# Moving transposes from TensorE to a DMA queue in a fused attention and expert kernel

**Chip, cores, metric.** One core of a Trainium2 chip. The time is device microseconds (us) of the core, the median of several executions. Engines are named as in the profile: PE (TensorE), PEld (its weight loads), DVE (VectorE), ACT (ScalarE), POOL (GpSimd), SP (SyncE, which here only issues DMAs). The profile gives the time of every DMA queue as a share of the same 16 DMA engines of the core.

## The reference

Pooled attention, then a routing by domain to eight experts. The result of the attention is the input of the experts.

```python
q_pool = q.reshape(B, H, S // 2, 2, D).mean(axis=3)        # B = H = 8, S = 1152, D = 64
scores = scale * np.matmul(q_pool, k.transpose(0, 1, 3, 2))
attn = softmax(scores)                                     # (cut: max, exp, sum)
x = np.matmul(attn, v).transpose(0, 2, 1, 3).reshape(4608, 512)
for e in range(8):
    mask = domain_id == e                                  # w1[e]: 512 x 1024, w2[e]: 1024 x 512
    out[mask] = np.maximum(x[mask] @ w1[e], 0.0) @ w2[e]
```

## The kernel before

Attention works on 32 pairs of heads. A pair is 12 steps; a step is one score block on PE (128 x 864) and its exponential on ACT. Keys and queries lie with tokens on partitions when they are loaded, and the kernel's score matmuls read them turned, so PE transposes them into PSUM and DVE copies them out:

```python
def turn_k(p):                       # eight key blocks; turn_q(p) does the ninth and six query blocks
    mt = tpsum.tile([P, 1024], F16, name="tp")
    for c in range(8):
        nc.tensor.transpose(mt[:, c * P : (c + 1) * P], in_=kp[:, c, :, :]..., identity=ident16[:, :])
    nc.vector.tensor_copy(kq[p][:, 0 : 8 * P], mt[:, :])
```

The main loop, one turn per step `t` (cut):

```python
p, s_ = divmod(t, SPP)                              # pair, step in the pair
if s_ == 0: load_q(p + 2)                           # SP's queue, 590 KB
if s_ in (2, 6): (load_k if s_ == 2 else load_v)(p + 3)   # GpSimd's software queue, cast to 16 bits
score(t); expo(t)
...                                                 # values of earlier steps, stores of x to DRAM
if s_ == 3: turn_k(p + 1)
if s_ == 7: turn_q(p + 1)
...                                                 # fills: expert tiles of 128 tokens where PE has room
if s_ == 8: prep_q(p + 2)                           # DVE: sum of the query pairs
if s_ == 11: prep_k(p + 2)                          # DVE: reorder
if t in WANT: want_weights(WANT.index(t))           # four experts' weights, 2.1 MB each
```

Rows of x go to DRAM, are gathered by expert (GpSimd), transposed by PE, and multiplied. There are 40 such tiles; 6 are done inside attention, 34 in a tail after it, in runs of up to five tiles of one expert (a run of the tail is tiles that use the same weights, one after the other). In the tail, short runs (up to 512 columns) share one PSUM tile between two row blocks:

```python
if m > 512:       hp_ = hps.tile([P, 1024], FP32, name="hp")       # hps: two buffers
elif f % 2 == 0:  hb_ = hps.tile([P, 1024], FP32, name="hp"); hp_ = hb_[:, 0:512]
else:             hp_ = hb_[:, 512:1024]
```

The softmax here doesn't subtract the row's maximum and nothing guards it: scores larger than these inputs give would overflow.

## Time and profile before

| | before |
|---|---|
| time, median of 4 (range) | 475.20 us (473.92 to 476.79) |
| attention ends (last exponential) | 319.5 us |
| last matmul of the tail | 466.3 us |
| tiles inside attention / in the tail | 6 / 34 |

The prediction below shows the busy shares, the slices and the waits.

### The profile page before, as it was taken

The page shows a single profiled execution, that of the slowest core. Times are in us where ns is not written, and L with a number is a line of the kernel's source. Part 1 is how long each engine was busy: PE and PEld are TensorE (multiplying, and loading weights), DVE is VectorE, ACT ScalarE, POOL GpSimd, SP SyncE. Part 2 cuts the span into 40 slices and gives each one's busy share as a digit, 9 for nine tenths or more (in the row PEclk, how much of TensorE's full clock was granted, in tenths as well). Part 3 has the DMA queues.
Part 4 walks back from the last instruction along what each step waited for, and adds up shares of the span by engine and source line. Part 5 has one row for each costly group of instructions (what it writes and reads, how often), then busy time and mean ns, then how long its engine had stood idle before and what let it go on. Part 6 is the DMA issues. An engine that isn't in the chain of part 4 may idle for free.

```text
span 473.8 us, 13280 instructions
## 1 busy us (share of the span) xinstructions
PE 443.1 (94%) x5683; PEld 313.9 (66%) x5683; DVE 227.8 (48%) x572; ACT 348.0 (73%) x459; POOL 161.4 (34%) x271
## 2 busy tenths in 40 slices
PE   7999999999999999999999999996888879999993
PEld 4777777877877877777787787773444445555551
DVE  4488778876454554554455454433222223232230
ACT  3999999999999999999999999991222223223220
POOL 4311231222611304564512432003336675533313
PEclk9999999999999999999999999998999999999998
DMA  9995699999999788599978666003219999912203
GB/s 204 219 245 90 129 240 221 183 260 189 167 244 227 121 201 185 100 200 276 244 124 207 138 120 150 1 25 96 80 58 169 217 222 222 232 58 84 81 16 109
DMA packets 48904, 75.23 MB, mean 159 GB/s; under 512 B 5567, under 2 KB 35008, under 8 KB 48834
## 3 DMA queue, kind: packets, MB, share of 16 engines
q0 software_dynamic: 35056, 50.05, 55.2%
q1 hardware_dynamic: 13186, 23.83, 18.6%
q8 instruction: 46, 0.75, 0.7%
q10 hardware_dynamic: 592, 0.39, 0.3%
q14 instruction: 24, 0.20, 0.1%
HBM read 95.46 MB, written 15.21 MB: 234 GB/s over the span
## 4 chain that ended last, share of the span: by engine, by line
ACT 52%; PE 26%; issue 11%; POOL 6%; DMA 3%; DVE 1%; POOLq 1%; ACTq 0%
ACT e L599 49%; PE s L587 8%; PE hp L1010 5%; PE op L1031 4%; PE acc L610 4%; POOL out_dram L504 4%; DMA w2h<-in_moe_w_dram 3%; ACT hT L1015 2%; PE m L763 1%; POOL xs L648 1%; PE m L776 1%; PE tp L550 1%; PE xp L985 1%; PE tp L564 0%; PE acc L161 0%
## 5 line engine op out<-in xcount | busy, mean ns | idle before, releaser
L599 ACT ACTIVATE e<-s 128x864 f16<-128x864 f32 x384 | 305.8, 893 | 4.7 <-PE s L587 3.9
L587 PE MATMUL s<-qz,kq 128*128 128x432 f16 (+2 forms) x1152 | 202.9, 284 | 5.6 <-ACT e L599 3.7
L610 PEld LDWEIGHTS <-e 128*128 128x128 f16 x2880 | 120.6, 97 | 24.7 <-DVE xb L624 7.8
L610 PE MATMUL acc<-v,e 128*128 128x65 f16 x2880 | 134.2, 193 | 0.3 <-ACT e L599 0.3
L587 PEld LDWEIGHTS <-kq 128*128 128x128 f16 x1152 | 97.9, 97 | 30.6 <-issue 10.2
L504 POOL DMA_INDIRECT out_dram<-osb,gid x40 | 40.2, 1004 | 102.9 <-ACT osb L1037 46.4
L648 POOL DMA_INDIRECT xs<-x_tok,grow x40 | 42.1, 1053 | 73.3 <-DVE xs L92 48.7
L1010 PE MATMUL hp<-xt,w1h 128*128 128x128 f16 (+3 forms) x384 | 57.7, 303 | 8.9 <-ACT hT L1015 8.9
L112 POOL DMA_DIRECT2D vs<-in_v_dram x32 | 23.9, 745 | 116.3 <-DVE v L529 57.1
L1031 PE MATMUL op<-w2h,hT 128*128 128x512 f16 x272 | 63.4, 379 | 0.0
L1010 PEld LDWEIGHTS <-w1h 128*128 128x128 f16 x416 | 35.9, 98 | 41.2 <-issue 17.5
L1015 ACT ACTIVATE hT<-hp 128x384 f16<-128x384 f32 (+2 forms) x36 | 20.7, 574 | 49.5 <-PE hp L1010 49.4
L1017 DVE TENSOR_SCALAR hT<-hp 128x384 f16<-128x384 f32 (+2 forms) x36 | 23.8, 661 | 65.1 <-PE hp L1010 63.6
L571 DVE COPY qz<-tp 64x576 f16<-64x576 f16 x62 | 28.2, 455 | 55.1 <-PE tp L564 51.1
L1037 ACT COPY osb<-op 128x512 f32<-128x512 f32 x21 | 12.3, 586 | 55.7 <-PE op L1031 50.0
L1031 PEld LDWEIGHTS <-hT 128*128 128x128 f16 x272 | 25.4, 98 | 25.2
L623 DVE RECIPROCAL rr<-acc 128x10 f32<-128x10 f32 x32 | 7.1, 221 | 48.1 <-PE acc L610 48.0
L520 DVE TENSOR_TENSOR qp<-q 96x768 f16<-96x768 f32 x31 | 29.3, 946 | 0.0
L624 DVE TENSOR_TENSOR xb<-acc,rr 128x640 f16<-128x640 f32 x32 | 26.4, 824 | 1.1
L1039 DVE COPY osb<-op 128x512 f32<-128x512 f32 x13 | 9.0, 692 | 35.5 <-PE op L1031 26.7
L121 POOL DMA_DIRECT2D k<-in_k_dram x31 | 23.3, 752 | 6.6 <-DVE q L92 3.6
L554 DVE COPY kq<-tp 128x1024 f16<-128x1024 f16 x31 | 21.2, 684 | 2.8 <-PE tp L550 2.7
(134 smaller groups left out, 323.2 us busy)
## 6 DMA issues: line engine op xcount, KB each, us to landing
q<-in_q_dram SPq DMA_DIRECT2D x30, 576.0 KB
vs<-in_v_dram POOLq DMA_DIRECT2D x32, 288.0 KB
k<-in_k_dram POOLq DMA_DIRECT2D x31, 288.0 KB
w1h<-in_moe_w_dram POOLq DMA_DIRECT2D x16, 512.0 KB
w2h<-in_moe_w_dram POOLq DMA_DIRECT2D x16, 512.0 KB
x_tok<-xb SPq DMA_DIRECT2D x23, 96.0 KB
x_tok<-xb SPq DMA_DIRECT2D x22, 64.0 KB
q<-in_q_dram SPq DMA_DIRECT2D x4, 288.0 KB
```

What stands on the lines that cost most here:

```text
L112: nc.gpsimd.dma_start(vs[:, :, :, :], v[b, h : h + 2].rearrange("h (p c) d -> p h c d", p=P))
L504: ins = nc.gpsimd.indirect_dma_start(out=dst[:, :], out_offset=bass.IndirectOffsetOnAxis(ap=ap, axis=0), in_=src, in_offset=None, **kw,)
L520: nc.vector.tensor_tensor(out=qp[:, :, :, :].rearrange("p j h d -> p h j d"), in0=q2[:, :, :, 0:D], in1=q2[:, :, :, D : 2 * D], op=ALU.add,)
L571: nc.vector.tensor_copy(qz[p % 2][r][lo : lo + 64, :], mt[lo : lo + 64, P : P + Sp])
L587: nc.tensor.matmul(s[:, r, o : o + n], lhsT=kq[p][:, c * P : (c + 1) * P], rhs=qz[p % 2][r][:, q0 : q0 + n], start=True, stop=True,)
L599: nc.scalar.activation(e_[:, :, o : o + W], st.pop(t)[:, :, 0:W], AF.Exp, bias=0.0, scale=0.0625)
L610: nc.tensor.matmul(acc[p][:, h, i * (D + 1) : (i + 1) * (D + 1)], lhsT=e_[:, h, o + QO[i] : o + QO[i] + P], rhs=v16[p % NV][:, c, h, 0 : D ...
L624: nc.vector.tensor_tensor(out=xb[b][:, :, 2 * hp * D : 2 * (hp + 1) * D].rearrange("p i (h d) -> p h i d", h=2), in0=a[:, :, :, 0:D], in1= ...
L648: nc.gpsimd.indirect_dma_start(out=dst, out_offset=None, in_=x_dram[0 : 1 + nb * Sp, :], in_offset=bass.IndirectOffsetOnAxis(ap=ap, axis=0),)
L1010: nc.tensor.matmul(hp_[:, lo : lo + n], lhsT=w1h[:, cc, f * P : (f + 1) * P], rhs=xt[:, cc, lo : lo + n], start=cc == 0, stop=cc == ND - 1,)
L1015: nc.scalar.activation(hT[:, f, 0:m], hp_[:, 0:m], AF.Relu)
L1031: nc.tensor.matmul(op_[:, :], lhsT=hT[:, f, i * P : (i + 1) * P], rhs=w2h[:, f, :], start=f == 0, stop=f == NF - 1,)
```

## The change

The intent: take all transposes after the first pairs off PE and its PSUM, use the room for more expert tiles inside attention, hold a fifth expert's weights for them, start sooner, and let short runs of the tail have a PSUM tile per row block. The core of the diff:

```diff
-    NFX = 20
+    NFX = 14
+    PT = 10
-    wpool = ctx.enter_context(tc.tile_pool(name="wpool", bufs=4))
+    wpool = ctx.enter_context(tc.tile_pool(name="wpool", bufs=5))
@@ transposes by SP's queue: keys (128x1152), queries (96x768), rows (128x512)
+    def flip_k(p):
+        new_kq(p)
+        nc.sync.dma_start_transpose(kq[p]..., kpt[p]...)
+    def flip_q(p):
+        qs[p] = qss.tile([P, Sp], F16, name="qs")
+        nc.sync.dma_start_transpose(qs[p]..., qpt[p]...)
+    def put_q(p, r):
+        nc.vector.tensor_copy(qz[p % 2][r][lo : lo + 64, :], qs[p][lo : lo + 64, :])
+    def flip_x(dst, e, i):
+        nc.sync.dma_start_transpose(dst, xs[e, i][:, :])
-    HELD = 4
-    WANT = [66, 100, 134, 230]
+    HELD = 5
+    WANT = [54, 84, 110, 140, 240]
@@ main loop
-        if main and p + 1 < NPAIR:
+        if main and PT <= p + 1 < NPAIR:
+            if s_ == 1:
+                flip_k(p + 1)
+            if s_ in (3, 4):
+                put_q(p + 1, s_ - 3)
+        if main and p + 1 < min(NPAIR, PT):
             if s_ == (6 if p == 0 else 3):
                 turn_k(p + 1)
@@
             prep_q(p + 2)
+            if p + 2 >= PT:
+                flip_q(p + 2)
@@ fills use two PSUM banks from pair PT; the tail
-        tc.tile_pool(name="hps", bufs=2, space=bass.MemoryType.PSUM, reuse_waits="tile")
+        tc.tile_pool(name="hps", bufs=3, space=bass.MemoryType.PSUM, reuse_waits="tile")
...
+            for j in range(j0, j1):
+                flip_x(xt[k_ + 1][:, :, (j - j0) * P : (j - j0 + 1) * P], en, j)
@@ cut: identity built before GpSimd's first loads, later loads of pair 1, pool bookkeeping, order of runs
```

## The prediction

> **What bounds the kernel now.** I read the page first: busy shares, then the 40 slices.
>
> ```profile
> PE 443.1 (94%) x5683; PEld 313.9 (66%) x5683; DVE 227.8 (48%) x572; ACT 348.0 (73%) x459; POOL 161.4 (34%) x271
> ...
> PE   7999999999999999999999999996888879999993
> ...
> ACT  3999999999999999999999999991222223223220
> ...
> DMA  9995699999999788599978666003219999912203
> ```
>
> The 94% of PE hides two stages. Up to slice 27 (320 us) ACT is full as well; after it ACT is at 2 and PE works alone. So there are two clocks: attention, paced by ACT's exponentials, and a tail of expert matmuls, paced by PE. DMA is full in much of both.
>
> ```profile
> L599 ACT ACTIVATE e<-s 128x864 f16<-128x864 f32 x384 | 305.8, 893 | 4.7 <-PE s L587 3.9
> ...
> L554 DVE COPY kq<-tp 128x1024 f16<-128x1024 f16 x31 | 21.2, 684 | 2.8 <-PE tp L550 2.7
> ```
>
> 384 exponentials (12 per head pair, 32 pairs). They overlap in the pipe; in the timeline those of pairs 1 to 10 start every 785 ns, those of pairs 11 to 30, where PE also fills in expert tiles, every 812 ns on average. 384 x 0.785 = 301 us is the floor of that stage, which lasts from 9.2 to 319.5 us. The start (timeline):
>
> ```profile
> 5.62 0.23 DVE L170 CAST ident<-ident 128x128 f16<-128x128 f32 x1 [2.99 <-POOL ident masks.py:199]
> ...
> 5.86 1.12 DVE L682 TENSOR_TENSOR qp<-q 96x384 f16<-96x384 f32 x2
> ...
> 9.23 0.89 ACT L599 ACTIVATE e<-s 128x864 f16<-128x864 f32 x1 [0.30 <-PE s L587]
> ...
> 11.49 4.80 ACT L599 ACTIVATE e<-s 128x864 f16<-128x864 f32 x6 [1.36 <-PE s L587]
> ```
>
> DVE stands 3 us behind the identity, which GpSimd builds after two loads; the query sum queues behind it, and the second exponential comes 2.3 us after the first where 0.8 would do. Now one run of the tail with three tiles (timeline) and the sum of its waits (list of waits, 320 us to the end):
>
> ```profile
> 343.86 1.46 PE L1010 MATMUL hp<-xt,w1h 128*128 128x384 f16 x8 [0.58 <-ACT hT L1015]
> ...
> 345.36 0.49 ACT L1015 ACTIVATE hT<-hp 128x384 f16<-128x384 f32 x1 [1.55 <-PE hp L1010]
> ...
> 345.90 1.46 PE L1010 MATMUL hp<-xt,w1h 128*128 128x384 f16 x8 [0.58 <-ACT hT L1015]
> PE hp L1010 <- ACT hT L1015: 11.2, 20, 0.6
> ```
>
> Short runs put two row blocks in one PSUM tile, so PE stops 0.58 us at every second block, 20 times, for ACT's eviction. The tail runs 319.97 to 466.32 us (last matmul), 146.3 us. It holds 272 / 8 = 34 tiles of 128 tokens. A tile costs 3.50 us: the last run, of five tiles and without transposes, takes 448.83 to 466.32. So 34 x 3.50 = 119.0 are work; transposes cost 0.22 us a tile in the chain, 34 x 0.22 = 7.5; finishing a started tile 1.7; the other 18 are waits (the 11.2 above, 3 for the first transposes one after the other through one bank, 1.7 from a half-rate clock of PE at 326 us).
>
> [...] between 360 and 410 us the software queue alone fills 111% of the 16 engines' time at 217 GB/s, and between 70 and 90 us the hardware queue gets 8%. [...] the gathers issued at 327.5 us deliver at 329 to 330.
>
> **The change part by part.** (a) *Keys and queries of pairs 10 to 31.* 22 pairs x (9 x 56 + 6 x 45 ns = 0.77 us) of TensorE transposes go, 17 us. PE does not set the pace there, so this is room, not time. DVE loses the PSUM copies (684 + 2 x 455 + 225 ns a pair) and gets two SBUF copies. (b) *Filled tiles.* The room, with the transposes of gathered rows gone and two PSUM banks for the fills, goes to expert tiles. The instruction order of the changed kernel shows 88 instead of 48 matmuls of the filling down projection: 11 tiles instead of 6. PE's load, with 360 ns for a score step, 310 for ten value matmuls and 213 for four fill matmuls (all spacings of the trace), was 8.68 to 8.90 us per pair and becomes 9.03, below 12 x 0.785 = 9.42. But a step with score, values and fill is 883 ns, and in the trace each such step lets the next exponential slip by 45 to 75 ns. There will be six a pair instead of three or four, though no 787 ns step with key transposes next to them, which made the worst slips. I take 812 ns a step as before: no gain, no loss. (c) *Start.* The identity comes before GpSimd's loads, so the query sum waits for its data, about 1 us earlier; the rest of the keys is transposed after the second score, which does not need it. First exponential at about 8, the second 0.8 later: up to 2.8 us; pair 0 has other heavy steps, so I take 2.3. Attention ends at 319.5 - 2.3 = 317.2. (d) *Tail.* 40 - 11 = 29 tiles x 3.50 = 101.5. No transposes (-7.5). Three PSUM tiles of two banks, one per row block, end the 0.58 us stops: a three-tile block takes PE 0.64 us and its eviction 0.5 to 0.6, on two engines in turn. The first run's rows lie transposed already (-3). Finishing the open tile is two matmuls, with the last values 1 us.
>
> New waits in the tail, which I estimate. The second run needs rows of the last batch: written, gathered, then transposed by DMA. Before, the gathers came 6.4 us after the last value eviction (321.1 to 327.5) and landed 2.5 us later[...]. Then five runs of 2, 2, 2, 3, 2 tiles pass in 7 to 10.5 us each. GpSimd needs in a two-tile run 2 gathers x 1.35 + 2 scatters x 1.15 + 4 weight loads x 0.78 = 8.1 us against 7, and gathers stand behind 2.1 MB of weights, 9.7 us at 217 GB/s. By that count the rows of the first five-tile run are transposed near 375 where PE is ready at 371: 4 us lost. Sum: 317.2 + 1 + 101.5 + 7 = 426.7 for the last matmul, + 7.5 for the last eviction, scatter and end (466.3 to 473.8 now) = 434.2 span, + 1.4 for time over span (475.19 to 473.8) = 435.6. I add 1.4 for late transposes in attention: **437 us**.
>
> **The rivals.** *The hardware queue is late.* A key transpose (128x1152, 295 KB) is let go when the pair before the last has freed its buffer and must land 11 steps, 8.6 us, later; it stands behind a query load of 590 KB. A query transpose has about five steps, 4 us. [...] if the 16 engines are full of weights, which now come earlier and for five experts, or the queue takes several us per transpose, DVE stops in front of the query copy and PE in front of the keys. One us on each of 22 pairs gives 459; three would undo the gain. For it: the full DMA digits. Against it: the digits are 6 to 8 in slices 20 to 24 and 0 to 3 in 25 to 30. *PE becomes the bound of attention.* Six slips of 75 ns and DVE's delays would give 830 ns a step: 18 ns x 252 steps, 4.5 us more, 442. *The tail is fed too late.* If a transposing DMA of 128x512 takes 4 us, five in a row take 20 against 17.5 us of a five-tile run and all three such runs pay: about 450. *Everything hidden*: no new wait in the tail and 800 ns a step give 427.
>
> **Range and chances.** The five tiles (17.5 us), the transposes (7.5) and the PSUM stops (11) are nearly certain and give 36 us, 7.6%, before any new wait. To lose to within 2% of 475.19 (over 465.7), the new waits would have to eat 28 us more than I count. The DMA risk lies above, so the range is wider there: 427 to 452. Faster by over 2%: 0.93; within 2%: 0.05; slower: 0.02.
>
> **What would show it.** ACT's full slices should end near 317 us, with the first two exponentials under 1 us apart at 8 to 9 us (c) and steps near 812 ns from pair 11 (b). The list of waits should have no DVE copy of qz and no score waiting for a transposing DMA beyond a few us in sum. In the tail, the waits of hp for hT should be gone, five-tile runs near 17.5 us, and any PE gap should stand before the second and the sixth or seventh run, ended by a transposing DMA. I am wrong if exponentials wait for keys or queries in many pairs, if steps exceed 830 ns, or if a 128x512 transposing DMA takes over 3.5 us.

The sum came to 426.7 us for the last matmul and to 437 in all. The reckoning of one term in it is cut: its 7 us of new waits are 3 before the second run, which rested on such a time, and the 4 that still stand, an estimate that holds a transposing time too. The 1.4 us for late transposes were a margin of mine and come from no measurement. What the trace did show of transposes is PE's: 219 ns for one of 128x128, eight in a row in 0.61 us.

## More of the kernel before

One more view turned out to matter, and I had asked for it only as coarse digits: the windows, one row for each stretch of time. Columns: window and length, then busy us (and instructions) of PE, PEld, DVE, ACT, POOL, then PE's granted clock, the mean busy share of the 16 DMA engines, and GB/s.

```profile
112.00:200.00 88.00, 86.90 (x1397) 68.76 (x1394) 46.36 (x101) 87.30 (x111) 27.52 (x41) 1.00 0.87 174
200.00:240.00 40.00, 39.68 (x627) 31.21 (x624) 21.31 (x50) 39.50 (x50) 19.65 (x29) 1.00 1.11 233
240.00:280.00 40.00, 39.19 (x616) 30.86 (x614) 20.43 (x47) 39.25 (x50) 12.86 (x21) 1.00 0.72 151
280.00:320.00 40.00, 38.90 (x640) 30.98 (x638) 16.98 (x36) 38.95 (x49) 5.15 (x10) 1.00 0.28 63
```

Read the last but one column. It is the time that packets took as a share of 16 engines, and passes 1 in the second row (1.11); I take 1 as full. From 112 to 240 us, which is pairs 10 to 23, 1 - share is worth 88 x 0.13 - 40 x 0.11 = 7 us of free DMA time in 128. From 240 to 320 us it is 11 + 29 = 40 us. What counts as full is not sharp: if the second row's 1.11 is full, the free times are 21 and 49 us. ACT (the fourth busy figure) is full in every window, so in the kernel before this traffic is just hidden.

## The result, and the profile after

| | before | predicted | after |
|---|---|---|---|
| time, median | 475.20 us | 437 (427 to 452) | 522.71 us (517.07 to 529.28, 4 runs, one of them slow) |
| pair 1 starts | 20.9 us | 18.6 | 19.0 us |
| attention ends | 319.5 us | 317.2 | 379.7 us |
| attention end to last matmul | 146.9 us | 109.5 | 127.8 us |
| tiles in attention / tail | 6 / 34 | 11 / 29 | 11 / 29 |

The kernel became 10% slower: ratio 1.096, 95% interval 1.086 to 1.106. Ratios here are the mean time of one kernel's fast runs over that of the other's of the same rounds, so not quite the ratio of the medians quoted. The profiled execution of the changed kernel took 517.07 us and was a fast one.

First the page: busy shares, then ACT's, the clock's and the DMA engines' rows in 40 slices (here of 12.9 us).

```profile
PE 427.9 (83%) x5306; PEld 298.0 (58%) x5306; DVE 199.9 (39%) x515; ACT 340.8 (66%) x443; POOL 161.9 (31%) x271
...
ACT  5999999839667897949907789799951210222230
PEclk9999999969888998979968999999999985999998
DMA  9996999996999999998999999999225699975112
```

Up to slice 7, counted from 0 (about 100 us), ACT is as full as before. From there, where pair 10's first transpositions run, it has holes to the end of attention, which moves from 27.0 to 29.5 slices of which each is longer, and DMA is at 8 or 9 from slice 10 to 27. PE's clock drops in some of the same slices. Next the groups that answer to those of before, with idle time and its releaser at the right end:

```profile
L622 ACT ACTIVATE e<-s 128x864 f16<-128x864 f32 x384 | 309.3, 893 | 62.3 <-PE s L610 61.3
L610 PE MATMUL s<-qz,kq 128*128 128x432 f16 (+2 forms) x1152 | 210.7, 293 | 30.3 <-DMA kq<-kp 22.4
...
L522 DVE TENSOR_TENSOR qp<-q 96x768 f16<-96x768 f32 x31 | 29.5, 951 | 39.3 <-DMA q<-in_q_dram 39.1
...
L577 DVE COPY qz<-qs 64x576 f16<-64x576 f16 x44 | 13.5, 308 | 27.1 <-DMA qs<-qp 26.4
```

The exponentials waited 4.7 us before and wait 62.3 now, each for its score. Scores wait for transposed keys, DVE's copies wait for transposed queries, and DVE's sums wait for the *loads* of the queries, whose code nobody touched. In the kernel before these sums waited for nothing:

```profile
L520 DVE TENSOR_TENSOR qp<-q 96x768 f16<-96x768 f32 x31 | 29.3, 946 | 0.0
```

The load's code is the same, but not its time of issue. In the trace SP's issues keep the program's order (query transposition, query load, key transposition, pair after pair from 92 to 358 us), and SP now stands at transpositions until source or buffer is ready (from 92 to 380 us, 47.4 us in 18 waits at keys for PE's scores and 50.0 in 11 at queries for DVE). In the traces a query load of pairs 11 to 31 is issued a median 17.3 us before the sum that uses it in the kernel before, and 8.1 us in the changed one.

The windows of the same stretches:

```profile
112.00:200.00 88.00, 71.13 (x1004) 52.53 (x1005) 30.45 (x76) 68.11 (x84) 20.70 (x30) 0.91 1.07 188
200.00:240.00 40.00, 35.30 (x491) 26.81 (x492) 14.33 (x34) 31.18 (x38) 14.23 (x22) 0.88 1.00 169
240.00:280.00 40.00, 27.28 (x377) 19.57 (x374) 11.05 (x28) 24.98 (x32) 14.93 (x24) 0.83 1.14 217
280.00:320.00 40.00, 36.55 (x533) 27.09 (x531) 17.34 (x37) 35.75 (x45) 9.80 (x16) 0.96 1.00 184
```

All four are full of DMA now, also the two that had 40 us free, and they move only 169 to 217 GB/s. PE's granted clock, 1.00 before, falls to 0.83 in one window. In this trace ACT is idle for 61 us between the start of pair 1 and the end of attention: in 39 of them PE is idle too, and in 15 PE works with its clock at half. e1, which has no such stalls, has no such time at half clock in attention (1.00 granted in each window from 10 to 317 us), so in these traces the low clock comes with the stalls; but it makes part of the loss. What fills the windows with DMA is in the page's table of queues (packets, MB, share of 16 engines over the span); first before, then after:

```profile
q0 software_dynamic: 35056, 50.05, 55.2%
q1 hardware_dynamic: 13186, 23.83, 18.6%
```

```profile
q0 software_dynamic: 35056, 50.05, 52.9%
q1 hardware_dynamic: 74898, 38.95, 39.2%
```

SP's hardware queue q1 took 18.6% of 473.8 us, 88 us of all 16 engines, and takes 39.2% of 515.2, 202 us. It gained 61,712 packets and 15.1 MB: 245 bytes a packet. So the transposes, with what they add to the queue's other packets, cost 114 us of DMA time, where I had only set the transfer time of each one against its deadline. How long one takes from issue to landing, with what stands ahead of it in the queue, shows in the chain of waits between 92 and 150 us (start, length, what; pieces between are left out):

```profile
92.79 7.63 DMA qs<-qp
...
100.49 12.45 DMA kq<-kp
...
138.93 16.43 DMA kq<-kp
```

I had taken less for each, a figure that no run showed. The traces also have transpositions with the engines to themselves: in e7, keys took 1.57 us (322.19 to 323.76 us, 188 GB/s; from issue to landing 4.3 us at the least in that run) and queries 0.89 (174.31 to 175.20 us, 166 GB/s). Beside the software queue it is another matter: between 148 and 154 us of the changed kernel that queue's packets take 92.2% of the 16 engines' time and move 0.94 MB, and q1, in these 6 us one key transposition, takes 29.9% and moves 0.24 MB, 40 GB/s.

In the tail, the timeline of PE shows two of the stops that I expected, at the first transposed run and at a later one:

```profile
395.83 2.36 PE L1020 MATMUL hp<-xt,w1h 128*128 128x256 f16 x20 [3.29 <-DMA xt<-xs]
...
433.54 7.88 PE L1020 MATMUL hp<-xt,w1h 128*128 128x384 f16 x32 [15.22 <-DMA xt<-xs]
```

The second is 15.2 us instead of 4.

### The profile page after: what moved, and what is told of

The parts are those of the page before. It is cut to its first block, busy times and chain, and to the rows that moved or that the text cites. A ratio compares the mean times of both kernels' runs of the same rounds, so it can differ in the third digit from the quotient of the medians.

```text
span 515.2 us, 12612 instructions
## 1 busy us (share of the span) xinstructions
PE 427.9 (83%) x5306; PEld 298.0 (58%) x5306; DVE 199.9 (39%) x515; ACT 340.8 (66%) x443; POOL 161.9 (31%) x271
## 3 DMA queue, kind: packets, MB, share of 16 engines
q1 hardware_dynamic: 74898, 38.95, 39.2%
## 4 chain that ended last, share of the span: by engine, by line
DMA 33%; ACT 24%; PE 21%; issue 11%; POOL 6%; DVE 2%; SPq 1%; POOLq 1%; ACTq 0%; DVEq 0%
ACT e L622 23%; DMA kq<-kp 12%; PE s L610 10%; PE acc L633 6%; DMA w2h<-in_moe_w_dram 5%; DMA xt<-xs 5%; DMA qs<-qp 4%; POOL out_dram L506 4%; DMA q<-in_q_dram 3%; DMA xs<-x_tok,grow 2%; DMA x_tok<-xb 2%; POOL xs L671 1%; PE tp L795 1%; SPq L662 1%; PE hp L1020 1%
## 5 line engine op out<-in xcount | busy, mean ns | idle before, releaser
L622 ACT ACTIVATE e<-s 128x864 f16<-128x864 f32 x384 | 309.3, 893 | 62.3 <-PE s L610 61.3
L610 PE MATMUL s<-qz,kq 128*128 128x432 f16 (+2 forms) x1152 | 210.7, 293 | 30.3 <-DMA kq<-kp 22.4
L633 PEld LDWEIGHTS <-e 128*128 128x128 f16 x2880 | 125.4, 100 | 28.8 <-DVE xb L647 10.0
L633 PE MATMUL acc<-v,e 128*128 128x65 f16 x2880 | 139.4, 196 | 0.4 <-ACT e L622 0.3
L1020 PE MATMUL hp<-xt,w1h 128*128 128x256 f16 (+3 forms) x352 | 49.6, 301 | 21.1 <-DMA xt<-xs 19.2
L1020 PEld LDWEIGHTS <-w1h 128*128 128x128 f16 x384 | 34.3, 100 | 44.5 <-issue 21.3
L1025 ACT ACTIVATE hT<-hp 128x256 f16<-128x256 f32 (+2 forms) x36 | 18.4, 514 | 53.9 <-PE hp L1020 46.9
L1038 PE MATMUL op<-w2h,hT 128*128 128x512 f16 x232 | 51.5, 379 | 0.0
L1027 DVE TENSOR_SCALAR hT<-hp 128x256 f16<-128x256 f32 (+2 forms) x36 | 21.1, 587 | 68.6 <-PE hp L1020 60.6
L522 DVE TENSOR_TENSOR qp<-q 96x768 f16<-96x768 f32 x31 | 29.5, 951 | 39.3 <-DMA q<-in_q_dram 39.1
L795 PEld LDWEIGHTS <-w1h 128*128 128x128 f16 x352 | 24.2, 101 | 16.8 <-issue 12.1
L795 PE MATMUL tp<-xt,w1h 128*128 128x128 f16 x176 | 17.9, 229 | 11.4 <-DMA xt<-xs 11.4
L577 DVE COPY qz<-qs 64x576 f16<-64x576 f16 x44 | 13.5, 308 | 27.1 <-DMA qs<-qp 26.4
```

What stands on the lines that cost most here:

```text
L522: nc.vector.tensor_tensor(out=qp[:, :, :, :].rearrange("p j h d -> p h j d"), in0=q2[:, :, :, 0:D], in1=q2[:, :, :, D : 2 * D], op=ALU.add,)
L610: nc.tensor.matmul(s[:, r, o : o + n], lhsT=kq[p][:, c * P : (c + 1) * P], rhs=qz[p % 2][r][:, q0 : q0 + n], start=True, stop=True,)
L622: nc.scalar.activation(e_[:, :, o : o + W], st.pop(t)[:, :, 0:W], AF.Exp, bias=0.0, scale=0.0625)
L633: nc.tensor.matmul(acc[p][:, h, i * (D + 1) : (i + 1) * (D + 1)], lhsT=e_[:, h, o + QO[i] : o + QO[i] + P], rhs=v16[p % NV][:, c, h, 0 : D ...
L795: nc.tensor.matmul(m[:, f % 4, :], lhsT=wts[e][0][:, cc, f * P : (f + 1) * P], rhs=h0["xt"][:, cc, :], start=cc == 0, stop=cc == ND - 1,)
L1020: nc.tensor.matmul(hp_[:, lo : lo + n], lhsT=w1h[:, cc, f * P : (f + 1) * P], rhs=xt[:, cc, lo : lo + n], start=cc == 0, stop=cc == ND - 1,)
```

## The experiments

Two questions were open: which part of the change costs the 60 us in attention, and why. For the why there were two theories. **L, lateness**: the bandwidth would do, but each transposition lands a few us after its deadline, behind others in SP's queue. **T, throughput**: the DMA engines have not the time for it all. L has a second form, **order**, for which no run was made: a transposition in SP's queue holds up the issue of what follows, such as the next query load. All kernels give a correct result except where said. "Attention ends" is from each run's profile. With one core, a run is called slow when it is over 1.5% above the kernel's fastest. In e5, e10 and e15 the profile fell on a slow run, so their ends, and what is read from their traces, are somewhat high, and I take their fast runs' times. Kernels e5 to e11 and e14 to e16 hold four experts, which frees room for buffers.

| run | what | attention ends | time, median us | ratio to before |
|---|---|---|---|---|
| e1 | all keys, queries on PE | 317.1 | 463.27 | 0.979 |
| e2 | no weight loads in attention | 366.2 | 508.11 | (one fast run, 503.75) |
| e3 | fill rows on PE | 385.6 | 525.29 | 1.110 |
| e4 | DMA from pair 24 | 336.1 | 477.79 | 1.009 |
| e5 | four experts held | 383.5 (slow) | 533.48 | 1.121 |
| e6 | e5, more slack | 417.0 | 568.37 | 1.197 |
| e7 | e5, no key/value loads | 341.1 | 499.69 | 1.048 |
| e8 | e5, keys only by DMA | 361.5 | 513.54 | 1.082 |
| e9 | e6, query load earlier too | 372.0 | 526.06 | 1.110 |
| e10 | PE transposes + unread DMA ones | 384.3 (slow) | 537.08 | 1.110 |
| e11 | PE transposes + unread plain copies | 347.0 | 503.81 | 1.061 |
| e12 | e1, gathers before weights, in part | 319.2 | 463.56 | 0.980 |
| e13 | e1, nearly all gathers first | 317.3 | 457.79 | 0.969 |
| e14 | e10 without the unread DMAs | 318.6 | 477.17 | 1.011 |
| e15 | e10, pairs 10 to 23 only | 368.8 (slow) | 522.01 | 1.102 |
| e16 | e10, pairs 24 to 31 only | 328.3 | 492.65 | 1.043 |
| e17 | e13, rows turned a run earlier | 316.6 | 455.73 | 0.959 |

### Which part: e1 to e4

**e1**, the change without DMA transposes of keys and queries:

```diff
-    PT = 10
+    PT = 32
-    want += [(e, 2, 308) for e in range(E)]
+    want += [(e, 2, 308) for e in [HELD - 1] + [x for x in range(E) if x != HELD - 1]]
```

> Keys and queries of all pairs stay on TensorE (PT = 32); gathered rows still go through the transposing DMA; five held experts. By the instruction order it fills 6 tiles, so 34 are left for the tail. Theory A (keys and queries land late behind the software queue's packets): attention ends near 318 us instead of 380, no score waits for a DMA, the tail takes 34 x 3.5 + 8 = 127 us, total 452 to 460. Rival B (row transposes in the fills and the earlier weights make attention late): attention still ends later than 340 and the total stays above 480.

Attention ends at 317.1 us, and the waits of the exponentials fall from 61.3 to 3.1 us. So the keys and queries are the cause of the loss in attention. The rest of the change, with 6 filled tiles, is about 2% faster than the kernel before (interval 0.964 to 0.993).

**e2**, the held experts' weights set by GpSimd in place of loads (a wrong result):

```diff
-        wqueue.extend(fns)
+        wqueue.extend([lambda: nc.gpsimd.memset(w[0][:, 0:2, :], 0.0), ...])
```

> Wrong result on purpose: the held experts' weights are memset by GpSimd instead of loaded, so 10.5 MB of software-queue traffic is gone from attention; everything else is the changed kernel. Theory A in its form 'weights in the same 16 engines delay the transposes': the pairs in which weights were loading (9 to 14, 18 to 22) drop from 900-1900 ns a step to 800-900, attention ends at 325 to 345 us, total 460 to 480. Rival C (the transposing DMA and the in-order SP queue are too slow by themselves): attention ends within 10 us of 380.

Attention ends at 366.2 us, 13.5 of some 60 us earlier: the weights take part, but they are not the cause alone. The figure is not clean: pairs 5 and 6 are slow in this run only (1046 and 894 ns a step against 785), some 4 us, probably since GpSimd spends 1.8 us on each memset in front of its loads. (The expectations of e5 say 10 us, from a first, wrong reading of this end.)

**e3**, the fills' rows turned on PE again, keys and queries still by DMA:

```diff
-            flip_x(h0["xt"][:, :, :], e, i)
+            mt = spare([P, ND, P], F16)
+            ...                                  # four PE transposes, one DVE copy
```

> Rows of the filled tiles turned by TensorE again, keys and queries of pairs 10 on still by DMA; 10 tiles are filled. Theory A: attention still ends at 360 to 380 us, total 505 to 520. Rival B (row transposes are what stalls PE in the fills): attention ends below 335 us, total below 475.

No gain. The row transposes inside attention are not what matters.

**e4**, DMA only from pair 24: `PT = 24` in place of 10.

> Transposing DMA for keys and queries only from pair 24, after the last held expert's weights are in; 9 tiles filled. Theory A: pairs 9 to 23 run at about 800 ns a step; pairs 24 to 31 lose what they lose in the changed kernel (about 7 us in sum) or less; attention ends at 320 to 330 us, tail of 31 tiles about 125 us, total 450 to 465. Rival C: the eight pairs lose 2 to 2.7 us each (60 us / 22.5 pairs), attention ends at 336 to 340.

Pairs 9 to 20 run at full speed, pairs 23, 24 and 26 to 29 lose 1 to 6 us each, and attention ends at 336.1 us, 17 us late and at the lower edge of rival C's range, although the last of the held weights is issued at 222 us, in pair 22.

### Why: e5 to e9

**e5** is the control for the next three: `HELD = 4`, `WANT` and four weight buffers as before.

> Control for the next three: the changed kernel with four held experts and four weight buffers as before, which frees 16 KB a partition; 9 tiles filled, 31 in the tail. The run without weights lost 10 us less in attention, so part of that: attention should end near 375 us (379.7 with five held), pairs 10 to 30 stay at 800 to 1900 ns a step, and two more tiles in the tail give about 520 us. All theories expect the same here.

Somewhat slower than the change and than I expected (the fast runs are 529 to 534 us), with two more tiles in the tail.

**e6**, more time for both transpositions, nothing else:

```diff
-            if s_ == 1:
-                flip_k(p + 1)
-            if s_ in (3, 4):
-                put_q(p + 1, s_ - 3)
+            if s_ in (9, 10):
+                put_q(p + 1, s_ - 9)
@@ after prep_k(p + 2), step 11
+            if p + 2 >= PT:
+                flip_k(p + 2)
@@ kqs: 3 buffers, qss: 2
```

> e5 with more time for both transpositions and no other work: keys are let go a pair earlier (third buffer, right after their conversion, 13 steps ahead instead of 11), and DVE puts the queries down at steps 9 and 10 instead of 3 and 4 (second buffer; 13 steps after they are let go instead of 7). Theory L (each transposition lands a few us too late, and the bandwidth would do): the waits go, attention ends at 318 to 325 us and the time is 460 to 468. Theory T (the 16 engines cannot move a pair's loads and transpositions in 9.4 us): a queue that falls behind is not helped by an earlier start, attention still ends past 355 us and the time is above 500. In between, 330 to 345, would say that some pairs have the bandwidth and others not.

Neither: it got worse. The list of waits shows where the wait went:

```profile
DVE qp L522 <- DMA q<-in_q_dram: 135.0, 18, 14.8
```

(us in total, times, longest.) Keys and queries now were in time, and the query load, issued right behind a key transposition in the same queue and wanted 8 steps later, was late instead; DVE stood in front of it, and PE's scores stood 57.1 us for DVE's copies of queries. I had moved the wait, and could not yet say whether for want of time or for the order.

**e9** therefore gives the query load a pair more as well:

```diff
-        if main and s_ == 0 and 1 < p and p + 2 < NPAIR:
-            load_q(p + 2)
+        if main and s_ == 0 and 0 < p and p + 3 < NPAIR:
+            load_q(p + 3)
```

> e6 again without what I take for its own fault: there the query load, issued after the key transposition and wanted 8 steps later, was what exponentials waited for. Here every query load is issued a pair earlier too, so loads and both transpositions have more than a pair (9.4 us) in hand. Theory L: attention ends at 318 to 330 us. Theory T: the engines' time is short by tens of us whatever the order, attention ends at 360 to 400 us.

Attention ends at 372.0 us. By the program's order everything now has more than a pair in hand (as issued, keys a median 13.2 us before their first exponential, the least 5.8), and the loss stays above 50 us. The groups again name the keys, which are let go 13 steps before their use:

```profile
L610 PE MATMUL s<-qz,kq 128*128 128x432 f16 (+2 forms) x1152 | 211.7, 294 | 40.0 <-DMA kq<-kp 32.0
```

The query loads are now issued a median 14.9 us before use, and from pair 11 on DVE waits 0.5 us for them in all. And the engines have no room left in any stretch (windows as before):

```profile
112.00:200.00 88.00, 74.81 (x1085) 54.99 (x1084) 33.55 (x77) 73.38 (x93) 21.42 (x30) 0.94 1.14 182
200.00:240.00 40.00, 30.28 (x444) 22.54 (x440) 12.75 (x32) 30.61 (x39) 18.58 (x28) 0.91 1.05 182
240.00:280.00 40.00, 28.92 (x396) 21.75 (x397) 11.73 (x27) 25.31 (x31) 12.19 (x19) 0.83 1.20 205
280.00:320.00 40.00, 30.46 (x424) 21.79 (x423) 11.61 (x29) 32.04 (x41) 10.18 (x16) 0.93 1.22 184
```

So more lead alone does not help: theory L in its plain form falls.

**e7** takes away other traffic instead: no loads of keys and values from pair 12 on (wrong result).

```diff
     def load_k(p, gate=False):
+        if p >= PT + 2:
+            loaded.setdefault(p, {})["k16"] = kvfix[1]     # a constant tile; load_v likewise
+            return
```

> e5 without the software queue's loads of keys and values from pair 12 on (a constant in their place, so a wrong result on purpose): 590 KB a pair, 512 packets, go; transpositions, their order and their deadlines stay. Theory T, and likewise the theory that the packets of a transposition alternate with those of the software queue: the waits go, attention ends at 318 to 328 us, keys transpose in 2 to 3 us from the start of their packets. Theory that the chain on SyncE's queue (query load, sum, transposition, one after the other) is too slow in itself: pairs still take over 900 ns a step, attention ends past 345 us.

In between: the end is 341.1 us (first exponential 2.6 us later than elsewhere). But the steps divide cleanly. Pairs 14 to 18 and 22 to 30 take 782 to 817 ns a step, with transpositions and fills; pairs 9, 12, 13, 20 and 21 take 972 to 1691. Weights are called for at steps 100, 134 and 230, so the slow pairs from 12 on are those in which they arrive. Without the software queue's bulk loads the transpositions keep up; beside them, whether keys and values or weights, they do not. SP's order is the same in all these pairs, so the order alone does not cause the loss.

**e8** leaves the queries on PE: `flip_q` and `put_q` go, six transposes and two copies of `turn_q` come back at step 7.

> e5 with only the keys transposed by DMA from pair 10; the queries go through TensorE and DVE as before, fills have one bank. Two thirds of the transposed bytes stay. If the loss follows the bytes (T), attention loses two thirds of e5's 55 us or somewhat less, so ends at 340 to 360 us; if the queries' short deadline (7 steps) starts the waits (L), it ends at 318 to 328 us. PE has 0.3 us of transposes a pair more than e5, which is room.

361.5 us, just past the range I gave T. The loss in attention, 43 us against e14's 318.6, is about two thirds of e5's 65 (slow), and in the time of fast runs it is 33 us of 52 (ratios 1.082, 1.121 and e14's 1.011): it goes with the bytes.

### A test of T with nobody waiting: e10, e11, e14 to e16

**e10** turns keys and queries on PE as before, and lets SP issue the same transpositions into scratch tiles that nobody reads. No exponential can wait for a transposition.

```diff
+        if main and 10 <= p + 1 < NPAIR and s_ == 1:
+            kd = dums.tile([P, KW], F16, name="kd")
+            nc.sync.dma_start_transpose(kd..., kpt[p + 1]...)
@@ after prep_q(p + 2)
+            if p + 2 >= 10:
+                qd = dums.tile([P, Sp], F16, name="qd")
+                nc.sync.dma_start_transpose(qd..., qpt[p + 2]...)
```

> Keys and queries of all pairs go through TensorE as before, rows by DMA, four experts held, 6 tiles filled; in addition SyncE issues the same transpositions from pair 10 on into scratch tiles that nobody reads. No exponential can wait for a transposition. Theory L: attention ends at 318 to 325 us, time 464 to 472. Theory T: the loads of keys, values and queries come late in their place, DVE waits for q or k, attention ends at 340 to 385 us and the time is above 485.

**e14** is e10 without these lines.

> The baseline of e10 and e11 without any scratch traffic: keys and queries on TensorE, four held experts. All theories: attention ends at 317 to 321 us, time 462 to 468.

Attention of e14 ends where expected (318.6 us); its tail is some 10 us longer than I expected, with 22.3 us of stops for transposed rows, one more expert's weights being loaded there. e10's fast runs are 523.6 and 529.3 us against e14's 477: about 47 us of loss (ratios 1.110 and 1.011) though no engine waits for the results of the added work. What waits is the query load. One wait and the queue's row of e10, then the same row of e14:

```profile
DVE qp L523 <- DMA q<-in_q_dram: 66.1, 14, 12.9
...
q1 hardware_dynamic: 74898, 38.95, 40.0%
```

```profile
q1 hardware_dynamic: 35474, 29.21, 26.2%
```

40.0% of 543.0 less 26.2% of 474.4 is 93 us of all 16 engines for 22 pairs, 4.2 us a pair, for 39,424 packets of 247 bytes on average. (This is a slow run, and the difference holds whatever longer the queue's other packets took. The same difference in e16, a fast run, is 3.7 us a pair.)

So the loss needs nobody waiting for results. But e10 is less direct a test of T than I meant it to be, since the scratch transpositions hold up SP's queue too: the query loads are issued a median 8.3 us before use here and 14.9 in e14. The form "order" is thus left in it. Against order alone stand e7 (same order, no loss where the software queue is quiet), e9 (loads as early as in e14, loss above 50 us, engines full) and e11, next. T holds by these; how the 47 us of e10 split between the two is not shown, since no run put the scratch transpositions behind the loads.

**e11**: the same bytes in plain copies, `nc.sync.dma_start(kd, kpt[p + 1])` and likewise for queries.

> e10 with plain copies of the same bytes between the same partitions (packets of some 1 to 2 KB instead of 256 bytes) in place of the scratch transpositions. If bytes are what fills the engines, the loss is that of e10; if it is the 256-byte packets [...], the loss is under half of e10's, attention ends under 335 us.

(By e10's row against e14's a packet took about 93 x 16 / 39,424 us, 38 ns of one engine.)

```profile
q1 hardware_dynamic: 41106, 38.95, 32.3%
```

32.3% of 502.6 less e14's 124.3 is 38 us: 5,632 packets of 1,729 bytes for the same 9.74 MB. The transposing form costs 2.4 times as much DMA time by e10's slow run, 2.1 times by e16's 3.7 us a pair. SP's order is that of e10 and the query loads are issued as late (a median 8.1 us before use), yet the loss is half (24 us by the ratios 1.061 and 1.011, against 47), so about half of e10's goes with the form of the transfers. It is not below half, and attention ends at 347 rather than under 335: even 38 us find no room. Plain copies alone would have cost time here.

**e15** and **e16** restrict e10's lines to pairs 10 to 23 and to pairs 24 to 31.

> e10 with the scratch transpositions in pairs 10 to 23 only. Account: the transpositions cost 4.4 us of all 16 engines a pair (q1's time in e10, 217.2 us, less e12's 120.6, over 22 pairs), 14 pairs 62 us; the kernel before has 7 us of DMA time free between 112 and 240 us. So the loss should be near 55 us of e10's 65: attention ends at 365 to 378 us. If instead the loss follows the number of pairs (65 x 14/22 = 41), it ends near 360.

> e10 with the scratch transpositions in pairs 24 to 31 only. Account: 8 x 4.4 = 35 us, and some 27 us of DMA time are free from 240 us to the end of attention: the loss should be near 8 us, attention ends at 323 to 332 us. If the loss follows the number of pairs (65 x 8/22 = 24), it ends near 342.

e15's ends lie within the range named (368.8, a slow run), and its fast runs lose 43 us against e14 (ratios 1.102 and 1.011): nearly all of e10's 47, where there were 7 us of free time (21 with 1.11 as full) and the number of pairs would give 30. e16's attention ends 9.7 us after e14's, as the account had it. But its pairs 24 to 31 lose 13.4 us, 3.7 more, since e14 happened to lose that much in pair 21, and its time is 15 us longer (ratios 1.043 and 1.011), where the number of pairs would give 17 of e10's 47: the 24 of my expectation came from e10's slow run. So e15 shows that the loss follows the free DMA time, and e16 by itself decides nothing.

One thing stays open: after 240 us the windows show 40 us free and 8 pairs need 29 (31.4% of 489.0 less 124.3), so a pure sum would hide them. That they still lose 13 us, in pairs 25, 26, 28 and 30 (957 to 1239 ns a step), may come from when the free time falls or from the order in SP's queue; no run separates that.

### The tail: e12, e13, e17

**e12** is e1 with gathers ahead of weights in the software queue:

```diff
-        h = stage1(..., {1: get, 4: get, 6: get} if n < NTC else {1: get, 3: get, 5: get})
+        h = stage1(..., {f: get for f in (1, 2, 3, 5, 6)})
+        while todo and todo[0][0] <= k_ + 2:
+            fetch(k_ + 2)
         if i1 == NTC and rest:                       # the next expert's weights
```

> e1 (keys and queries on TensorE throughout, the rest of the change kept; 463.27 us, best of what was tried) with one edit in the tail: five gathers in the first block of each run instead of three, and all gathers of the run after next issued before the next expert's weights. If the 10.1 us in front of the first five-tile run in e1 are gathers standing behind weights, they go and the time is 451 to 455 us. If the transposing queue itself is late there, it stays at 461 to 465.

A miss. The stop is unchanged:

```profile
378.61 8.49 PE L1020 MATMUL hp<-xt,w1h 128*128 128x512 f16 x32 [10.12 <-DMA xt<-xs]
```

Its last gathers were still issued (at 364 and 365 us) after two experts' weights, since my lookahead of two runs did not reach them.

**e13** looks five runs ahead (`k_ + 5` in place of `k_ + 2`, 28 row buffers).

> e12 with all remaining gathers looked ahead five runs instead of two and a pool of 28 row tiles, so nearly all of them (17 of 20) stand before the first expert's weights on the software queue. In e12 the last two gathers of the stopped run were issued at 363.8 and 365.1 us, behind 4.2 MB of weights issued from 346.4 us on (19 us at 217 GB/s), and PE stopped 10.1 us. If that is the cause, this stop goes, and the time is 451 to 456 us. If transposing itself is late, it stays at 461 to 465.

457.79 us, a little short of what I expected; the stop moves and halves:

```profile
396.74 9.94 PE L1020 MATMUL hp<-xt,w1h 128*128 128x128 f16 x60 [4.93 <-DMA xt<-xs]
```

So half of this stop was gathers behind weights. PE's stops for transposed rows in all fall less, from 12.0 us in e1 to 9.5.

**e17** adds a third buffer for transposed rows, lets a run's transpositions go one run earlier, and calls the fifth expert's weights at step 272 instead of 240.

> e13 with a third buffer for transposed rows in the tail, so the transpositions of a run are let go one run (10 to 17 us) earlier, and the fifth expert's weights from step 272 instead of 240, where the engines are no longer full. If the remaining 4.9 us are the late start of transpositions, they go, and pair 21 (960 ns a step in e13) falls to 800, 2 us: 449 to 453 us. If they are the queue's pace, the tail keeps its stops and only the 2 us show: 455 to 457.

The 4.9 us go, and the only stop for rows left is 2.95 us before the second run. Another comes instead, where PE waits for a freed output bank:

```profile
409.32 3.57 PE L1039 MATMUL op<-w2h,hT 128*128 128x512 f16 x8 [4.79 <-ACT osb L1045]
```

The step of pair 21 falls from 960 to 796 ns, and that of pair 22 rises from 792 to 915, so the later weights move the loss more than they end it. The time is the second of the two that I had named, though the stop tied to it went. At 455.73 us, ratio 0.959 (0.956 to 0.963), e17 is the fastest kernel and beats both: the change's start, tail and row transposes, with keys and queries left on PE.

## Why the prediction was wrong

**The step that failed** is the weighing of the first rival, "The hardware queue is late". I named it, set times that no run had shown against its deadlines, and wrote "Against it: the digits are 6 to 8 in slices 20 to 24 and 0 to 3 in 25 to 30" and so "I add 1.4 for late transposes in attention". That term measured 61 us (379.7 against 317.2 + 1.4). Three things were wrong in it. First, the digits were read in the wrong place: the transpositions begin at 93 us, in slice 7 counted from 0, and the digits are 9 up to slice 12. Of slices 25 to 30 only 25 and 26 lie in attention at all, and slice 30 reads 9. From 112 to 240 us the engines had 7 us free in 128, or 21 with 1.11 as full. Second, I never added up engine time, nor saw that SP's order would delay the query loads (issued 17.3 us before use in the kernel before, 8.1 in the changed one). Latency against deadline was the wrong measure; e9 shows that more lead helps little (526 us against e5's 533), and e10 that no wait for a transposition is needed for the loss. Third, the size: a pair needs more than the figure I took, 2.5 us alone (e7) and 3.5 (the change) to 4.2 (e15, slow) beside the other traffic, so 14 pairs need 50 to 58 us. The text even held the key: it read off the trace that the software queue alone filled 111% of the 16 engines' time (360 to 410 us of the kernel before), and drew no sum from it. One sum in it is off as well: over 22 pairs 1.7 us each, not three, would undo the gain of 38.

The account closes roughly. In the change, q1 gained 114 us; the 41 row transpositions are 36 of them (e14's 124 us less 88), keys and queries 78, or 3.5 a pair, less than in e10. Fourteen pairs are 50 us, the ten row tiles turned before pair 24 are 9, and between the starts of pairs 10 and 24 nine weight loads of 0.52 MB are issued instead of eight, 2 us at 217 GB/s; less the 7 free that is 54. Pair 24 started 54.5 us later than before (295.6 against 241.1), and 6 more were lost after it. The closeness is partly luck: with 21 us free the sum is 40, and it has no term for PE's half clock or for SP's order. A fixed loss per pair, which I used for this rival ("One us on each of 22 pairs gives 459; three would undo the gain"), would have been 2.7 us.

**(a), (b) room on PE**: right in count (11 tiles filled), and PE did not become the bound: in e7 the undisturbed pairs with transpositions by DMA and nine filled tiles run at 782 to 817 ns a step against 812 assumed. That rival falls. Eleven tiles at full speed were never seen.

**(c) start**: 2.3 us predicted, 1.9 measured at pair 1 (20.89 to 18.96). The exponentials run on without a gap after the first, at 8.57 us:

```profile
8.57 5.80 ACT L622 ACTIVATE e<-s 128x864 f16<-128x864 f32 x7 [0.51 <-PE s L610]
```

**(d) tail**: the mechanism was right and sizes were off. From the end of attention to the last matmul it takes 127.8 us, 19.1 fewer than before, where I had 109.5. The stops for PSUM evictions went (20 stops of 0.58 us before, one of 0.9 after), and the stop before the second run is 3.3 us where I had 3. The later one is the mis-sized term: 15.2 us where I had 4. By what e13 and e17 show of e1's stop, gathers stand longer behind weights in one queue than I counted, and transpositions then start late; in the changed kernel itself this was not tested. The same run's 32 matmuls then took 7.88 us instead of 5.4 (e1, e13), 2.5 us from a lower clock after the stop (0.68 granted from 433.5 to 441.5 us, 1.00 after), which I had not counted; stops of under 1 us make up 2.6 more.

Altogether 61 us in attention and 18 in the tail, 79 of the 80 us between the prediction and the profiled run's 517.07.

## What to carry to other kernels

Before moving work to a DMA queue, add up the busy time of the DMA engines in each stage, window by window, and compare it with the time that the new transfers will occupy there; this kernel, which hides its traffic behind ACT, had 7 us of 128 left from 112 to 240 us, and issuing the transfers earlier still lost over 50 us (e9). To tell lateness from lack of time, issue the same transfers with nobody waiting for them, but where they cannot hold up the issue of others, which e10 did not heed; and give everything more lead, as e9 did, and look whether any engine time is left. Where a wait moves to a load that nobody touched (here the queries'), look at two things: the shared engines, and whether the load is still issued as early as before.
